# Attention, then two mixture-of-experts layers, on one core: the first head pair in halves, unread products, one gather by indirect DMA, and reads and loads in another order

## The chip, the cores and the metric

The kernel runs on one core of a Trainium2 chip. The metric is the device time of one execution in microseconds; the figure for a kernel is the median of its runs. The engines are named as the profile names them: PE (matrix products; PEld are its weight loads), DVE (vector), ACT (activations), POOL (GpSimd), SP (starts most of the DMAs). Each runs its own list of instructions in the order in which it is written, and waits where an input is not there yet.

## The reference

Three stages follow each other; the output of one is the input of the next.

```
scores = q @ k.T / 8                          # B=2, H=8, S=576, D=64, f32
scores = where(i // 64 >= j // 64, scores, -1e9)
attn   = exp(scores - max) / (sum + 1e-9);  x = attn @ v       # rows of 8*64 = 512
# MoE 1: N=1152 rows, E=8 experts, F=1024, capacity 288: one expert per row
e = argmax(x @ w_gate); slot = rank of the row among those of e, kept if below 288
x = gate_w * (relu(disp @ w1[e]) @ w2[e]), back in the row's place, else 0
# MoE 2: two experts per row, by noisy logits
out = sum over the two of weight * (relu(x @ w1[e]) @ w2[e])
```

## The kernel before

**Attention.** The 8 heads of a batch go in pairs, so there are 8 pairs (`pr`), and a pair's 576 rows are cut into tiles of 128 (the last has 64 rows of both heads). `turn_ops` turns a pair's q and k around on PE (line 442, and 479 for the last rows), ACT writes the rounded half of each (450, 487), DVE the remainder (459, 456, 492), and a copy of the rounded half goes into the other 64 partitions (466 by DMA; for the first pair 468 on ACT and 470 on POOL). These lie in `W[pr % 2]`, the tiles `both`, with a part that stands for the mask. `tile_ops` makes scores (526, 531), maxima on DVE (537 to 542), exponentials on ACT (550, 552), turns them (562, 558), copies them out (421 on DVE or 423 on ACT) and multiplies with v (608, 623). `fin_ops` ends a pair: it divides by the sums, writes the rows (`xrow`, lines 664, 667, 702) and the pair's share of the router's logits (674 to 694).

**Router and first rows.** `gate_ops(b)` takes a batch's logits (`g0`, 739 to 748), counts ranks on PE (`gp`, 752 to 757), places the rows (763 to 773), and enters row numbers into the table `T1` by one-hot products (`cells1` 797, `table` 806, `keep` 810). The first 128 rows of expert 0 are taken without a DMA: for each of the 5 tiles of rows of both batches PE multiplies `xrow` with a one-hot `choice` (779), 4 products a tile (`rows_in`, 822); all add up in one bank, which ACT and DVE split (858, 859). All rows also go to `x_d` in DRAM (`store`, 405, 406): batch 0 in one piece, batch 1 in columns 0 to 383 and then the rest.

**Weights.** Each expert's weights come in 8 units of 512 KB through a few raw buffers (`load`, 156, 159, on SP's queue); `split` makes two halves of a unit, rounded on ACT (167) and remainder on DVE (170, two instructions). Eleven units are split inside the attention; a split frees its raw buffer, and the load of a later unit goes out behind it on SP. One unit per expert stays whole (`wf`).

**Order in the attention.** `Weave` is a planner that runs when the kernel is built: `add` enters operations with cost, dependencies and the buffers they take, and `run` simulates the engines and picks the next operation by a score with the weights in the table `ATT` (line 22) and a random tie-break (`seed`, `noise`). What it writes is each engine's order; on the chip only semaphores decide when things run. MoE stages have a planner of their own (`Flow`).

**MoE 1.** `row1(e, blk)` gathers up to 128 rows of expert `e` from `x_d` by an indirect DMA on POOL (1441), for experts 0 and 1 ahead of the loop, later from inside it. `prep` turns the rows (1015) and splits them (1018, 1021). Here expert 0 takes the branch for at most 128 rows (`one_block`), which reads its rows from the bank above, and of its gathered rows only the columns behind the data.

**MoE 2.** `arm(e)` computes two blocks of 128 rows of expert `e`, and beside them prepares the next: `next_rows` and `rows2` gather (1418) into `g`. The output is read back, added to and written again: `prev` (1577) is an indirect DMA from `out`, `to_out` adds (1583) and scatters (1586). At the end of the program's list the loop is:

```
    for e in range(1, E):
        for blk in range(2):
            prev(G[e, blk][1], blk)
        arm(e)
        if e + 1 < E:
            with tc.If(many["n"] > 256):
                rest(e)
```

`rest(e)` is run for experts with more than 256 rows; in the trace that is one of them.

## Time and profile before

| | |
|---|---|
| median of 3 runs | 559.38 us (557.72 to 559.82) |
| profiled execution: time, span | 557.14 us, 555.5 us |
| mean granted PE clock | 0.992 |
| PE busy | 517.0 us (93%) |
| DVE / ACT / POOL busy | 378.9 (68%) / 294.1 (53%) / 138.4 us (25%) |
| read from and written to DRAM | 87.5 and 12.3 MB, 180 GB/s |

The time of an execution is a little over its span, which counts from the first to the last instruction of the core. PE is the engine with the most work; from about 14 us on it is busy in nearly every slice of the page but the eleventh and the thirty-sixth, so what counts are the places at which PE stands still and the work that it need not do. The timeline gives start, duration, engine, line, operation, and in brackets how long the engine had been idle and what ended that.

### The profile page before, as it was taken

How to read it: one execution, taken by the hardware profiler on the slowest of the kernel's cores; microseconds unless marked ns; L12 is line 12 of the kernel's file. 1: busy time of each engine (PE TensorE's matmuls, PEld its weight loads, DVE VectorE, ACT ScalarE, POOL GpSimd, SP SyncE). 2: the span in 40 equal slices, each digit the busy share in tenths (PEclk: the TensorE clock that was granted, in tenths of full speed). 3: DMA queues.
4: the chain of work that ended last, by engine and by line, in shares of the span. 5: the costliest groups of instructions: out<-in, count | busy, mean ns of one | idle time of the engine just before them, and what ended most of it. 6: DMA issues, size and time to landing. Idle time of an engine off the chain costs nothing. (4 is left out here: it accounts for less than half of the span.)

```text
span 555.5 us, 10106 instructions
## 1 busy us (share of the span) xinstructions
PE 517.0 (93%) x3381; PEld 422.8 (76%) x3381; DVE 378.9 (68%) x1008; ACT 294.1 (53%) x580; POOL 138.4 (25%) x225
## 2 busy tenths in 40 slices
PE   3999999999869999999999999989999999969996
PEld 3778777878647776787976967888989886949794
DVE  7899988888548988757674678464848562917441
ACT  5888878871347687544533536252635442716130
POOL 3000000000462234405233133142513132514131
PEclk9999999999999999999999999999999999979999
DMA  6998896423458878754632442638658591545220
GB/s 136 221 240 229 220 230 188 123 77 109 137 176 290 265 240 296 232 189 138 206 133 64 170 137 71 226 125 284 221 205 280 188 327 48 187 180 165 86 66 35
DMA packets 71176, 99.17 MB, mean 179 GB/s; under 512 B 37130, under 2 KB 40586, under 8 KB 71088
## 3 DMA queue, kind: packets, MB, share of 16 engines
q1 hardware_dynamic: 63600, 83.16, 47.6%
q0 software_dynamic: 6432, 14.71, 8.4%
q8 instruction: 39, 0.64, 0.5%
q14 instruction: 49, 0.40, 0.2%
q10 hardware_dynamic: 1056, 0.26, 0.2%
HBM read 87.53 MB, written 12.25 MB: 180 GB/s over the span
## 5 line engine op out<-in xcount | busy, mean ns | idle before, releaser
L170 DVE TENSOR_TENSOR wl<-raw,wh 128x512 fp32r<-128x512 f32 x140 | 91.6, 685 | 12.0 <-ACT wh L167 11.6
L167 ACT ACTIVATE wh<-raw 128x1024 fp32r<-128x1024 f32 x70 | 71.1, 1052 | 20.1 <-PEq L1780 12.5
L170 DVE TENSOR_TENSOR both<-raw,both 128x512 fp32r<-128x512 f32 x100 | 66.0, 684 | 8.9 <-ACT both L167 8.4
L167 ACT ACTIVATE both<-raw 128x1024 fp32r<-128x1024 f32 x50 | 51.3, 1054 | 10.0 <-PEq L1780 8.3
L198 PE MATMUL h<-xh,wh 128*128 128x256 f32 (+1 forms) x184 | 52.9, 287 | 0.5
L199 PE MATMUL h<-xl,wh 128*128 128x256 f32 (+1 forms) x184 | 52.6, 286 | 0.0
L200 PE MATMUL h<-xh,wl 128*128 128x256 f32 (+1 forms) x184 | 52.5, 285 | 0.0
L1018 ACT ACTIVATE xh<-tp 128x512 fp32r<-128x512 f32 (+1 forms) x37 | 19.0, 536 | 59.0 <-PE tp L1015 57.3
L1021 DVE TENSOR_TENSOR xl<-tp,xh 128x512 fp32r<-128x512 f32 (+1 forms) x37 | 21.9, 610 | 35.3 <-ACT xh L1018 35.1
L1145 ACT ACTIVATE hh<-h 128x512 fp32r<-128x512 f32 (+1 forms) x46 | 24.1, 523 | 38.7 <-PE h L200 32.3
L1586 POOL DMA_INDIRECT out_dram<-o,T2i x16 | 18.5, 1156 | 96.9 <-DVE o L1583 94.8
L1148 DVE SCALAR_TENSOR_TENSOR hl<-h,hh 128x512 fp32r<-128x512 f32 (+1 forms) x46 | 27.5, 597 | 22.1 <-ACT hh L1145 18.0
L198 PE MATMUL h<-xh,both 128*128 128x256 f32 (+1 forms) x136 | 39.2, 288 | 2.7 <-DVE hl L1148 1.4
L199 PE MATMUL h<-xl,both 128*128 128x256 f32 (+1 forms) x136 | 39.0, 287 | 0.0
L200 PE MATMUL h<-xh,both 128*128 128x256 f32 (+1 forms) x136 | 38.8, 285 | 0.0
L198 PE MATMUL y<-wh,hh 128*128 128x512 f32 (+1 forms) x94 | 38.3, 407 | 0.0
L200 PE MATMUL y<-wh,hl 128*128 128x512 f32 (+1 forms) x94 | 37.1, 394 | 0.0
L199 PE MATMUL y<-wl,hh 128*128 128x512 f32 (+1 forms) x94 | 36.9, 393 | 0.0
L550 ACT ACTIVATE pt<-s,negmax 128x128 f32<-128x128 f32 (+3 forms) x64 | 33.4, 526 | 6.4 <-DVE negmax L537 5.1
L526 PE MATMUL s<-both 128*128 128x256 f32 (+2 forms) x128 | 33.1, 371 | 3.8 <-ACT both L468 2.5
L198 PEld LDWEIGHTS h<-xh,wh 128*128 128x128 f32 x184 | 34.7, 189 | 2.1 <-issue 1.6
L199 PEld LDWEIGHTS h<-xl,wh 128*128 128x128 f32 x184 | 34.6, 188 | 0.0
(295 smaller groups left out, 1297.9 us busy)
## 6 DMA issues: line engine op xcount, KB each, us to landing
raw<-in_moe_w_dram SPq DMA_DIRECT2D x120, 512.0 KB, 5.1
wf<-in_moe_w_dram SPq DMA_DIRECT2D x8, 512.0 KB, 5.8
out_dram<-zero SPq DMA_DIRECT2D x3, 768.0 KB, 5.5
both<-both SPq DMA_DIRECT2D x14, 160.0 KB, 2.6
raw<-in_q_dram SPq DMA_DIRECT2D x16, 128.0 KB, 4.2
vn<-in_v_dram SPq DMA_DIRECT2D x16, 128.0 KB, 2.6
both<-both SPq DMA_DIRECT2D x14, 144.0 KB, 3.3
raw<-in_k_dram SPq DMA_DIRECT2D x14, 128.0 KB, 4.7
```

What stands on the lines that cost most here:

```text
L167: nc.scalar.activation(h, t, AF.Copy)
L170: (nc.gpsimd if part == 3 else nc.vector).tensor_sub(l[:, c], t[:, c], h[:, c].bitcast(F32))
L198: nc.tensor.matmul(o, sh, mh, start=first, stop=False)
L199: nc.tensor.matmul(o, sh, ml, start=False, stop=False)
L200: nc.tensor.matmul(o, sl, mh, start=False, stop=last)
L526: nc.tensor.matmul(o, w[:, i, h, 128 * t:128 * t + 128], w[:, i + 2, h, 64 * h:64 * h + n], start=(i == 0), stop=(i == 1))
L550: nc.scalar.activation(o, i, AF.Exp, bias=negmax[:, pr, 2 * t + h:2 * t + h + 1], accum_out=ssum[b][:, t, 2 * p + h:2 * p + h + 1])
L1018: nc.scalar.activation(xh[:, :, c0:c0 + n], h["tp"][:, :, :n], AF.Copy)
L1021: nc.vector.tensor_tensor(xl[:, :, c0:c0 + n], h["tp"][:, :, :n], xh[:, :, c0:c0 + n].bitcast(F32), op=OP.subtract)
L1145: nc.scalar.activation(part(hfull[0], g - (KF - 2 * WHOLE) // per) if plain(g) else part(hh, g), of(g), AF.Relu)
L1148: nc.vector.scalar_tensor_tensor(part(hl, g), of(g), 0.0, part(hh, g).bitcast(F32), op0=OP.max, op1=OP.subtract)
L1586: ins = nc.gpsimd.indirect_dma_start(out=out, out_offset=_off(G[key][1][:n, 0:1]), in_=G[key, "o"][:n], in_offset=None, bounds_check=NT - ...
```

## The change

The table `ATT` has other weights and another seed, the planner's costs and lags are set anew, and so the whole order of the attention moves. Beside that:

- *First pair.* Its q and k are loaded in halves of 256 rows (k on SP, q on ACT's queue), turned, split and copied half by half; the copies run on ACT or DVE, none on POOL. Scores of the first two tiles need only the first halves. The masks come from a pattern that POOL writes directly, without two ACT instructions; most small constants are made on POOL.
- *Unread products.* 56 bf16 products of a tile of ones go to PE into a bank that nobody reads, ahead of and between the first pair's steps.
- *First rows.* Batch 0's part of expert 0's first 128 rows is fetched from `x_d` by an indirect DMA (it waits for the store and for the table of batch 0) and enters the bank by 4 products with the identity.
- *Late loads.* Loads of units from the sixth on wait behind the store of batch 1.
- *Gathers and reads.* `row1` runs in the order (1,0), (0,1), (0,2), (1,1), (1,2), (0,0). `prev` of MoE 2 enters the planner's list inside `arm`.

```diff
-ATT = dict(P=0.024, A=0, V=0.122, G=0.074, beta=0, fit=0.3348, seed=13885, noise=0.1383, ...
+ATT = dict(P=0.076, A=0.0803, V=0.2935, G=0.2811, beta=0, fit=0.4128, seed=81227, noise=0.1133, ...
+UNREAD = 56
...
-                    queue = max(queue, op["end"] + 1.3) + op["dma"]
-                    op["end"] = queue + 1.0
+                    queue = max(queue, t + 1.5) + op["dma"]
+                    op["end"] = max(queue, op["end"] + 1.3) + 0.7
...
+            if b == p == 0:
+                for c in range(2):
+                    for i, src, e in ((1, k, nc.sync), (0, q, nc.scalar)):
+                        for hh in range(2):
+                            e.dma_start(out=qn[:, i, 2 * c:2 * c + 2, hh, :], in_=src[b, hh, 256 * c:256 * c + 256, :].rearrange("(c p) d -> p c d", p=128))
...
-        for x, m in enumerate((-31.5, -95.5)):
-            nc.gpsimd.memset(mid[:, x:x + 1], m)
-            nc.scalar.activation(near[x], jq, AF.Square, bias=mid[:, x:x + 1])
...
+            for g in range(2):
+                for x in (1, 0):
+                    main(x, 2 * g, 2)
+                made["W", pr, g] = list(res)
             a2 = tail()
+            res.append(AT.add("dup", "AV", dict(A=0.9, V=0.7), dup_tail, [a2]))
...
-                S_ = AT.add("s", "P", cost, scores, made["W", pr], ["s"])
+                S_ = AT.add("s", "P", cost, scores, made["W", pr, t // 2] if t < 4 else made["W", pr], ["s"])
...
+                def at(op):
+                    nc.gpsimd.tensor_scalar(rows0_at, T1f[:, 0:1, 0], float(NT), None, op0=OP.add)
+
+                def fetch(op):
+                    nc.gpsimd.indirect_dma_start(out=rows0, out_offset=None, in_=x_d[0:S], in_offset=_off(rows0_at[:, 0:1]), bounds_check=S - 1, oob_is_err=False)
+
+                st = AT.add("load", "S", 0.9, lambda op: store(0, slice(0, XW)), rows + [wt, made["gates"]], dma=3.8)
+                i0 = made["at"] = AT.add("fetch", "G", 0.2, at, [made["keep", 0]])
+                made["fetch"] = AT.add("fetch", "G", 1.2, fetch, [i0, st], dma=1.5)
...
+            def early(op):
+                for kk in range(KD):
+                    nc.tensor.matmul(bank(op, "s").rearrange("p (k n) -> p k n", n=128)[:, kk], rows0[:, kk * 128:kk * 128 + 128], ident,
+                                     start=(kk == 0), stop=False)
...
-            made["raw", i + RAWS] = AT.add("load", "S", 0.1, lambda op: load(behind(u)), [made["split", i]], dma=1.5, drawn=False)
+            made["raw", i + RAWS] = AT.add("load", "S", 0.1, lambda op: load(behind(u)), made["split", i], dma=1.5, drawn=False, behind=[made["stored"]] if i >= HELD else ())
...
+        def unread(op):
+            nc.tensor.matmul(rings["av"][0][:, 0:128], ones, ones, start=True, stop=True)
...
-    for blk, n in BLK:
-        row1(0, blk, n)
-
-    for blk, n in BLK:
-        row1(1, blk, n)
+    for e, i in ((1, 0), (0, 1), (0, 2), (1, 1), (1, 2), (0, 0)):
+        row1(e, *BLK[i])
...
-        blocks(F, E + e, xT[e % 2], 0, lambda y, blk, p, first: to_out(F, y, (e, blk), blk, p, first), done=done, apart=e + 1 == E)
+        before_ = [F.add("G", 1.04, lambda blk=blk: prev(G[e, blk][1], blk), after=3.5 if e + 1 < E else 0.0) for blk in range(2)]
+        blocks(F, E + e, xT[e % 2], 0, lambda y, blk, p, first: to_out(F, y, (e, blk), blk, p, first, deps=[before_[blk]]), done=done, apart=e + 1 == E)
...
-        for blk in range(2):
-            prev(G[e, blk][1], blk)
         arm(e)
```

Past the attention PE, DVE and ACT have the same instructions in the same order; POOL's order differs in `row1` and in six of the seven arms, SP's not at all.

On PE, at the end of the attention, before: the products with `choice` of batch 0 (line 822, `xrow_125`) stand between the last pair's closing steps (674 to 687 and 652), one tile of rows (x4) or two (x8) at a time.

```order
L822 MATMUL s_201<-choice_223,xrow_125 128x128 x4
L674 MATMUL tp_205<-xt_218,wblk 32x128 x4
L675 MATMUL tp_205<-xt_218,wblk 32x64
L676 MATMUL tp_205<-s4s,eye_165 64x2
L677 MATMUL tp_205<-ident,xt_218 64x128
L822 MATMUL s_201<-choice_223,xrow_125 128x128 x4
L686 MATMUL tp_205<-ident,lt_186 128x128
L687 MATMUL tp_205<-ident,lt_186 64x32
L652 MATMUL tp_206<-ident,xt_217 128x128 x4
L652 MATMUL tp_204<-ident,xt_218 128x128 x4
L822 MATMUL s_201<-choice_223,xrow_125 128x128 x8
```

The same place of the changed kernel (its lines 695 to 708 and 673 are those steps):

```order
L695 MATMUL tp_201<-xt_214,wblk 32x128 x4
L696 MATMUL tp_201<-xt_214,wblk 32x64
L697 MATMUL tp_201<-s4s,eye_166 64x2
L698 MATMUL tp_201<-ident,xt_214 64x128
L673 MATMUL tp_200<-ident,xt_214 128x128 x4
L673 MATMUL tp_202<-ident,xt_213 128x128 x4
L707 MATMUL tp_201<-ident,lt_182 128x128
L708 MATMUL tp_201<-ident,lt_182 64x32
```

Nothing of batch 0's rows stands between these steps now; the table of batch 0 is entered just ahead of them, and the 4 products with the fetched rows stand behind the ranks of batch 1.

On SP, at the same place, before: `raw` is a weight load, `x_d` the store of the rows of batch 1 (`xrow_124`), `wf` the unit that stays whole.

```order
L159 DMA raw_68<-in_moe_w_dram 128x2x512
L156 DMA raw_69<-in_moe_w_dram 128x1024
L156 DMA raw_70<-in_moe_w_dram 128x1024
L405 DMA x_d<-xrow_124 128x4x384
L406 DMA x_d<-xrow_124 64x384
L156 DMA raw_71<-in_moe_w_dram 128x1024
L156 DMA raw_67<-in_moe_w_dram 128x1024
L405 DMA x_d<-xrow_124 128x4x140
L406 DMA x_d<-xrow_124 64x140
L159 DMA wf_1746<-in_moe_w_dram 128x2x512
```

And in the changed kernel:

```order
L406 DMA x_d<-xrow_122 128x4x384
L407 DMA x_d<-xrow_122 64x384
L406 DMA x_d<-xrow_122 128x4x140
L407 DMA x_d<-xrow_122 64x140
L158 DMA raw_68<-in_moe_w_dram 128x2x512
L155 DMA raw_69<-in_moe_w_dram 128x1024
L155 DMA raw_70<-in_moe_w_dram 128x1024
L155 DMA raw_71<-in_moe_w_dram 128x1024
L155 DMA raw_67<-in_moe_w_dram 128x1024
L158 DMA wf_1804<-in_moe_w_dram 128x2x512
```

All five loads stand behind the whole store; before, three stood ahead of its first piece and two more ahead of its second.

On POOL, in an arm of MoE 2, before: `px<-out_dram` are the two reads of `prev`, `g<-x_d` the gathers for the next block of rows, `out_dram<-o` the scatters.

```order
L1577 DMA px_1732<-out_dram,T2i 128x512
L1577 DMA px_1733<-out_dram,T2i 128x512
L1418 DMA g_1740<-x_d,T2i 128x524
L1418 DMA g_1741<-x_d,T2i 128x524
L1418 DMA g_1742<-x_d,T2i 32x524
L1386 TENSOR_LOAD cnt_92
L1586 DMA out_dram<-o_6630,T2i 1152x512
L1586 DMA out_dram<-o_6631,T2i 1152x512
```

And in the changed kernel:

```order
L1461 DMA g_1798<-x_d,T2i 128x524
L1461 DMA g_1799<-x_d,T2i 128x524
L1461 DMA g_1800<-x_d,T2i 32x524
L1617 DMA px_1790<-out_dram,T2i 128x512
L1617 DMA px_1791<-out_dram,T2i 128x512
L1429 TENSOR_LOAD cnt_90
L1626 DMA out_dram<-o_6688,T2i 1152x512
L1626 DMA out_dram<-o_6689,T2i 1152x512
```

The three gathers stand ahead of the two reads in the six arms that have gathers.

## Rows read from the trace of the kernel before

**Rows 1.** Windows: stretch, length, busy by engine (instructions), PEclk, DMA share, GB/s

```profile
0.00:20.00 20.00, 11.41 (x57) 9.74 (x57) 14.11 (x43) 12.88 (x30) 5.00 (x29) 1.00 0.68 145
20.00:120.00 100.00, 97.01 (x841) 76.64 (x839) 89.62 (x209) 84.83 (x231) 0.00 (x0) 1.00 0.75 197
120.00:141.28 21.28, 19.82 (x197) 16.89 (x194) 18.48 (x66) 6.00 (x16) 0.10 (x1) 1.00 0.39 122
141.28:162.00 20.72, 14.48 (x67) 10.38 (x68) 9.61 (x21) 6.78 (x11) 11.88 (x19) 1.00 0.47 151
```

**Rows 2.** Waits of PE: who waited for whom, us in total, times, longest

```profile
PE tp L1015 <- DMA g<-x_d,T2i: 5.0, 2, 4.6
PE tp L1015 <- DMA xr<-x_d,T: 4.4, 2, 2.3
...
PE tp L562 <- ACT pT L423: 0.4, 1, 0.4
```

**Rows 3.** Timeline of the first pair, 5 to 14 us, PE and ACT

```profile
5.39 1.94 PE L442 MATMUL tp<-ident,raw 128*128 128x128 f32 x8 [5.39 <-DMA raw<-in_k_dram]
6.52 1.20 ACT L450 ACTIVATE both<-tp 64x512 fp32r<-64x512 f32 x2 [1.87 <-PE tp L442]
...
7.80 0.57 ACT L487 ACTIVATE both<-tp 64x128 fp32r<-64x128 f32 x2
...
9.50 1.48 ACT L468 ACTIVATE both<-both 64x640 fp32r<-64x640 f32 x2
...
10.28 2.48 PE L526 MATMUL s<-both 128*128 128x256 f32 x8 [2.52 <-ACT both L468]
```

**Rows 4.** Timeline of PE, the same products of a later pair

```profile
110.85 1.21 PE L526 MATMUL s<-both 128*128 128x256 f32 x8
```

**Rows 5.** Groups of PE by line in 120 to 133 us: x, busy, mean ns

```profile
L822 PE MATMUL s<-choice,xrow 128*128 128x128 f32 (+1 forms) x40 | 5.4, 279 | 0.0
```

**Rows 6.** Timeline of the attention's end, PE

```profile
130.46 2.14 PE L822 MATMUL s<-choice,xrow 128*128 128x128 f32 x16
132.53 0.20 PE L752 MATMUL tp<-oh,before 128*128 128x48 bf16 x1
...
134.41 4.92 PE L822 MATMUL s<-choice,xrow 128*128 128x128 f32 x40 [1.21 <-DVE choice L779]
```

**Rows 7.** Timeline of DVE, the last step ahead of the ranks

```profile
131.69 0.20 DVE L748 TENSOR_TENSOR oh<-real,ix 128x40 bf16<-128x40 f32 x1
```

**Rows 8.** Timeline of SP, ACT, POOL and PE, from the store to the first gathers

```profile
139.77 0.51 SPq L406 DMA_DIRECT2D x_d<-xrow  x1
...
146.21 0.60 ACT L1043 ACTIVATE yT<-h 128x512 f32<-128x512 f32 x1 [6.23 <-DMA x_d<-xrow]
...
147.03 1.22 POOL L1441 DMA_INDIRECT xr<-x_d,T  x1 [4.32 <-DMA wf<-in_moe_w_dram]
...
151.12 1.02 POOL L1441 DMA_INDIRECT xr<-x_d,T  x1 [0.31 <-issue]
152.44 1.48 POOL L1441 DMA_INDIRECT xr<-x_d,T  x1 [0.30 <-DVE wl L170]
...
146.86 0.66 PE L1048 MATMUL tp<-ident,yT 128*128 128x128 f32 x4 [1.86 <-ACT yT L1043]
155.09 0.65 PE L1015 MATMUL tp<-ident,xr 128*128 128x128 f32 x4 [2.26 <-DMA xr<-x_d,T]
158.78 0.63 PE L1015 MATMUL tp<-ident,xr 128*128 128x128 f32 x4 [2.11 <-DMA xr<-x_d,T]
```

**Rows 9.** Timeline of POOL and PE in the arm behind `rest`

```profile
481.15 1.84 POOL L1577 DMA_INDIRECT px<-out_dram,T2i  x1 [4.31 <-DMA out_dram<-o,T2i]
...
485.08 1.46 POOL L1418 DMA_INDIRECT g<-x_d,T2i  x1 [0.32 <-issue]
...
493.06 1.12 PE L1015 MATMUL tp<-ident,g 128*128 128x128 f32 x4 [4.64 <-DMA g<-x_d,T2i]
```

**Rows 10.** Window of PE behind that wait

```profile
493.00:498.00 5.00, 4.62 (x14) 3.28 (x14) 1.38 (x2) 1.20 (x2) 0.00 (x0) 0.50 0.07 27
```

## What I predicted before the run

> **What bounds the kernel now.** I read the windows of the attention and of what follows it first, then the table of PE's waits, then the timeline of each place at which PE stands. In 20 to 120 us PE is busy 97.0 of 100 us, against 76.6 (weight loads), 89.6 (DVE) and 84.8 (ACT) [rows 1]: there another order can win at most 3 us. PE loses time elsewhere: 8.6 us of the first 20, 1.5 of 21.3 in the attention's end and 6.2 of the 20.7 behind it [rows 1]. The table of waits names 5.0 us for gathered rows `g` in MoE 2, one of the two waits being 4.6, and 4.4 us in two waits for gathered rows `xr` [rows 2]. So a change at these places moves the end nearly one for one: behind the attention the order on PE, DVE and ACT stays, and what PE wins early it keeps unless something else comes late.
>
> **The first pair.** Before, the first turn starts at 5.39, when the k data land, and the first scores at 10.28: 4.89 us, in which ACT makes k's rounded half (two of 1.20 overlapping), the tail, q's half and the copy, in a row [rows 3]. PE's last wait there, 2.52, ends with that copy on ACT. With halves of 256 columns an activation should take between the 0.57 of the pair with 128 columns and the 1.20 of that with 512; I take 0.78, an estimate. Three of these (k half, q half, one copy; the other copy may lie on DVE) and about 0.9 of turning and of latency give 3.3 where 4.89 stood: 1.6 won. The halves have half the bytes and may land 0.5 to 1 before the 5.39, an estimate; I take 0.5. The first score products, 8 in 2.48 us [rows 3], took 1.21 at a later pair [rows 4], half as long: PE was at half speed, after standing idle. If the unread products keep it awake, up to 1.27 come back for these and something for the turns. Against it: 1.38 us of POOL's copying goes to ACT and DVE, shorter instructions cost a fixed part more each, and the second halves still have to be done before the third tile. I take 0.4 for the speed net of all this. Term 2.5, between -1 (the added instructions lie on the path) and 5 (the whole of 4.89 but the shortest possible, and the speed).
>
> The granted clock column shows 1.00 for 0 to 20 us [rows 1] though the products took twice their time, so for the start I trust the durations. In the window behind the long wait it does read 0.50 [rows 10], that is 1.2 of 2.4 GHz, after 4.64 us of idleness. The Trainium skill ("TensorE: Matmul & The Clock Gate", Part 1) says that the throttled state is the default and that activity releases it, so that unread products would count as well as read ones; the trace of before agrees with the first half (half speed at the start) and has nothing on the second. By that rule alone the start would gain the 1.27 and some of the turns.
>
> The 56 unread products cost nothing as long as PE waits anyway: 128 columns in bf16 against the 128x128 f32 products of 279 ns [rows 5] are at most 56 x 0.28 = 15.7 us of busy time at the very worst, in truth a fraction, and the last 14 of them stand ahead of the third tile's scores, at most 1 us if nothing else holds it up. The masks and constants go to POOL, which is busy 5.0 of 20 us [rows 1]; this idleness hides them. If a constant is late, the turns are late by it: inside the bound of -1.
>
> **The end of the attention.** Ahead of the ranks of batch 1, 40 products with `choice` go, 5.4 us [rows 5]; 4 products of 128x128 f32 with the identity come in, 8 records in the trace's count; at the rate of the 40 in 4.92 us, 0.12 each, they take 1.0 [rows 6]. Saved on PE: 4.4. But PE is not alone there: the ranks' input on DVE ended at 131.69 + 0.20 = 131.89 [rows 7], and the ranks started at 132.53 only because 16 of these products were before them [rows 6]: 0.6 is certain. What stands earlier between the closing steps fills waits of PE for DVE and ACT, which then show up as idleness. And batch 1's own 40 products still wait 1.21 for `choice` on DVE [rows 6]. The new order takes DVE's work of batch 0's `choice` (two instructions) off and puts batch 0's table ahead of the closing steps. I take 1.2, nearer to the certain end; bounds -3 and 4.1. The lower one is the fetch: table, `keep`, POOL's index, indirect DMA. Such a gather takes 155.09 - 151.12 = 3.97 from its start to the product that uses it and 158.78 - 152.44 = 6.34 with loads beside it [rows 8]; if it ends last, PE waits.
>
> **Store, loads and first gathers.** Three waits follow: 1.86 (ACT's step waited until 146.21 for the store begun at 139.77), 2.26 for the fourth gather, issued at 151.12, and 2.11 for the fifth, issued at 152.44 [rows 8]. The store moves ahead of five loads. Before, it took 146.21 - 139.77 = 6.4 with loads ahead of it; 1.9 less removes the first wait, and the gathers start about as much earlier. The one for (1,0) was fourth and is now first: 151.12 - 147.03 = 4.1 earlier beside that, so the 2.26 goes. (1,1) goes from fifth to fourth: 1.3 + 2, so about 0.6 less its flight; I keep the third wait at 2.9 to be careful, that is 0.6 to 0.8 worse. Sum 1.86 + 2.26 - 0.6 = 3.5; bounds 0 and 6.2 (all three). Late next: the loads now all lie behind the store and beside the gathers; the unit `wf` and the units that expert 0 and 1 take are later by up to the time of the three loads that stood ahead.
>
> **MoE 2's reads.** In the arm behind `rest`, the reads of `prev` stand ahead of the gathers on POOL and the first waits 4.31 us, until 481.15, for a scatter to `out`; the first gather goes at 485.08 and PE waits 4.64 until 493.06 [rows 9], then runs at clock 0.50 in 493 to 498, busy 4.62 [rows 10], half of which, 2.3, is excess. In the changed order the gathers need not wait for that scatter: they can go from 481.15 - 4.31 = 476.84 on, 8.2 earlier, while PE needs them 4.64 earlier. So 4.64, another 0.4 of the second wait [rows 2] and 2.3 go: 7.4 (0 to 7.4). Now `prev` is late instead: its two reads, 3.9 us from 481.15 to 485.08, stand behind three gathers and are needed only when the last products of a block are added, some 10 us on. The other arms' gathers were in time (PE has only these two waits in the table) and stay so.
>
> **The body of the attention.** New weights and seed give a new order; PE was busy 97 of 100 us, so 0, bounds -2.5 and 3.0.
>
> **Sum.** 2.5 + 1.2 + 3.5 + 7.4 + 0 = 14.6; 557.14 - 14.6 = 542.5. The profiled execution was 2.2 below the median of the runs, 559.38; I add half of that: 543.6.
>
> **Rivals.**
> - The unread products don't raise PE's speed, and the last 14 hold up the third tile: 0.4 and 1.0 go, the start gives 1.1, so 545.0. For it: the granted clock shows nothing to win.
> - The late loads collide with the gathers and the weights of expert 1 come late: the third term falls to 0, 547.1. For it: 6.34 against 3.97 for a gather beside loads [rows 8]. In the skill ("DMA: Bandwidth & Descriptors", "Issuing engines are not separate DMA queues") transfers interleave on the same 16 engines whoever starts them, which speaks against gaining by POOL's queue alone; by that rule the time would be 547.1 too, and the longer flight agrees.
> - The gathers of the arm aren't what PE waits for, or start late for another reason: the fourth term falls to 0, 551.0. Against it: the timeline's 8.2 us of room.
> - The fetched rows end last: the second term is -2.8, so 547.6.
> - Slower: the new order brings the chain maxima, exponentials, turning and copying out of a tile closer to its products, so that PE waits in each of 7 tiles x 8 pairs. The one wait of this kind that shows in before is 0.4 [rows 2]; 56 x 0.4 = 22.4 over the 14.6 won gives 543.6 + 22.4 = 566. It comes out slower than before by more than 0.5% from (562.2 - 543.6) / 56 = 0.33 us a tile on. Against it: the numbers of score and turning buffers stay, and 89.6 and 84.8 of 100 us on DVE and ACT [rows 1] leave them some room.
>
> **How the numbers follow.** Forecast 0.55, its own range 537 to 549 (start and gathers at either end); the clock 0.10; the collision 0.12; late gathers 0.08; the fetch last 0.08; the slow order 0.04. The range for all is 537 to 551. A measurement of this kernel can tell about 0.5%: 556.6 to 562.2 counts as no change. Everything but the last rival is below it, and 0.03 is left for several of them at once, which would come out within the 0.5%: faster 0.93, same 0.03, slower 0.04.
>
> **What would show it.** The first scores start near 8 us and 8 of their products take 1.2 to 1.5; in the window of the attention's body PE stays at 96 or more of 100; between the closing steps PE has gaps in place of the products of batch 0, and the ranks follow DVE's last step within 0.2; the store's landing is no one's wait, one wait for `xr` is left; in the arm behind `rest` the wait for `g` is gone and the clock stays 1.00. It is wrong if PE waits over 3 us for the fetched rows, if waits for weight loads appear in the first experts, or if POOL is so late with `prev` that DVE's adding holds up PE.

## The result, and the profile after

The changed kernel takes 550.94 us (median of 4 runs, 545.85 to 551.55); the kernel before, with one more run beside these, 558.55 (4 runs, 555.88 to 559.82). The ratio is 0.9865 (95% interval 0.983 to 0.9899): 7.6 us faster, where 543.6 had been forecast. The direction held and the size was about half. The profiled execution took 550.74 us against 557.14, its span 549.1 against 555.5: 6.4 less.

Both spans can be cut at the same events and compared stretch by stretch (times in us; the marks are PE's rows in the two timelines):

| stretch | before | after | difference | forecast |
|---|---|---|---|---|
| start to the first pair's last score products | 20.01 | 19.48 | -0.53 | -2.5 |
| body: to the last pair's last score products | 98.06 | 105.83 | **+7.77** | 0 |
| end of the attention: to expert 0's first product | 23.21 | 22.18 | -1.03 | -1.2 |
| expert 0's whole unit `wf`, and the first gathers | 18.44 | 12.76 | -5.68 | -3.5 |
| MoE 1 and MoE 2 up to the arm behind `rest` | 295.70 | 296.28 | +0.58 | 0 |
| that arm to the next | 64.73 | 57.17 | -7.56 | -7.4 |
| rest of the program | 35.35 | 35.40 | +0.05 | 0 |

Three stretches gave 14.3 us, 12.1 had been forecast for them; the body took 7.8 back. The windows of the changed kernel, cut at these marks, show how (columns as in [rows 1]: length, then each engine's busy time and count for PE, PEld, DVE, ACT, POOL, then granted clock, DMA share, GB/s):

```profile
0.00:19.48 19.48, 14.91 (x114) 12.46 (x114) 15.22 (x36) 14.47 (x38) 8.60 (x42) 0.91 0.59 131
19.48:125.31 105.83, 99.44 (x823) 77.32 (x822) 87.53 (x213) 81.30 (x219) 0.00 (x0) 0.95 0.70 184
125.31:147.49 22.18, 19.20 (x177) 16.59 (x178) 17.80 (x65) 9.50 (x23) 1.52 (x3) 0.92 0.23 64
147.49:160.25 12.76, 12.03 (x58) 9.51 (x59) 8.63 (x20) 6.05 (x10) 7.64 (x9) 1.00 0.87 310
456.53:513.70 57.17, 56.70 (x353) 47.20 (x352) 33.26 (x56) 25.53 (x37) 23.08 (x16) 1.00 0.52 178
```

The same stretch of the body in the kernel before:

```profile
20.01:118.07 98.06, 95.07 (x826) 74.91 (x823) 87.77 (x206) 83.19 (x227) 0.00 (x0) 1.00 0.76 201
```

PE does the same products in both (823 and 826 records). It stood still for 6.39 us instead of 2.99, which is 3.40; and it was busy for 99.44 us instead of 95.07, which is 4.37, at a mean granted clock of 0.95 instead of 1.00. DVE and ACT did no more than before. So the 7.77 are idle time and the slow clock behind it, in about equal parts. A second trace of the changed kernel (below) has 107.75 for this stretch, 9.7 more than before.

PE's waits in the whole changed program (us in total, times, longest), against [rows 2]:

```profile
PE s L547 <- DMA both<-both: 3.9, 4, 1.8
PE sm L1388 <- DVE C L1383: 3.7, 8, 0.7
PE s L547 <- ACT pt L571: 3.3, 5, 2.2
PE tp L776 <- DVE oh L772: 2.4, 1, 2.4
```

The waits for `g` and `xr` are gone, all of them. New at the top are score products that wait for `both<-both`: the DMAs that copy the rounded half of a pair's q and k into the other 64 partitions. PE's timeline at the fourth pair (start, duration, engine, line, operation; in brackets how long PE was idle and what ended it):

```profile
55.45 0.21 PE L708 MATMUL tp<-ident,lt 32*64 32x32 f32 x1
57.47 0.58 PE L547 MATMUL s<-both 128*128 128x256 f32 x1 [1.80 <-DMA both<-both]
58.76 1.86 PE L547 MATMUL s<-both 128*128 128x256 f32 x7 [0.71 <-DMA both<-both]
```

Why the copies came late stands in the list of SP's queue (SPq: time that the sequencer spent letting out the DMAs, and how many):

```profile
41.32 4.18 SPq L320 DMA_DIRECT2D raw<-in_q_dram  x2
45.53 1.28 SPq L320 DMA_DIRECT2D raw<-in_k_dram  x2
47.34 0.69 SPq L322 DMA_DIRECT2D q<-in_q_dram  x1
48.08 0.62 SPq L322 DMA_DIRECT2D q<-in_k_dram  x1
48.80 2.08 SPq L324 DMA_DIRECT2D vn<-in_v_dram  x2
50.98 0.60 SPq L325 DMA_DIRECT2D vn<-in_v_dram  x1
51.68 0.54 SPq L158 DMA_DIRECT2D raw<-in_moe_w_dram  x1
52.31 2.46 SPq L467 DMA_DIRECT2D both<-both  x4
```

And ACT's last step of what they copy, from its timeline:

```profile
47.48 0.55 ACT L502 ACTIVATE both<-tp 64x128 fp32r<-64x128 f32 x2
```

The fourth pair's data were ready at 48.03; its copies left SP from 52.31 on, behind all the loads of the fifth pair and one of a weight unit, PE stood from 55.67 and went on at 57.47. In the kernel before the copies of this pair stood behind the fifth pair's loads too, but SP got through these by 48.65:

```profile
41.29 1.89 SPq L319 DMA_DIRECT2D raw<-in_q_dram  x2
48.74 2.47 SPq L466 DMA_DIRECT2D both<-both  x4
```

There ACT's last step ended at 48.63 and PE came for the copies only at 56.97, 8.2 after the first left SP. In the changed order this room is 3.4. So the place in the list is not new; what changed is that SP needs 10.9 us instead of 7.4 to let out what stands ahead of the copies (the first two loads alone 4.18 instead of 1.89), and that PE comes 1.3 earlier. Why SP needs longer is not shown; from 38.15 on it had let out three weight units and a store of 768 KB, in the kernel before one unit and one such store in that time. Then the clock: one window at the second pair, and two around this wait.

```profile
20.00:30.00 10.00, 8.55 (x62) 6.74 (x63) 6.46 (x15) 7.62 (x20) 0.00 (x0) 0.83 1.05 270
50.00:60.00 10.00, 7.44 (x61) 5.97 (x61) 6.12 (x16) 6.35 (x15) 0.00 (x0) 0.86 0.87 213
60.00:70.00 10.00, 9.76 (x62) 7.49 (x62) 7.93 (x16) 7.33 (x22) 0.00 (x0) 0.80 0.75 204
```

From 60 to 70 us PE is busy for 9.76 of 10 (9.48 in the kernel before), but does 62 products in it; the kernel before does 77, and two traces below without that wait 85 and 94. A busy PE hides the loss: only the clock column (0.80, part of the time at 1.2 of 2.4 GHz) and the count show it. Between the last score products of successive pairs (first to second, second to third, and so on) the kernel before takes 15.9, 12.3, 16.4, 13.2, 15.6, 12.5, 12.1 us; the changed one 17.0, 13.9, 18.5, 17.1, 13.1, 14.3, 12.0.

The start, on PE's timeline:

```profile
1.20 2.42 PE L906 MATMUL av<-ones 128*128 128x128 bf16 x21 [1.20 <-DVE ones L85]
7.21 1.35 PE L547 MATMUL s<-both 128*128 128x256 f32 x8
8.62 0.94 PE L906 MATMUL av<-ones 128*128 128x128 bf16 x14
11.81 0.62 PE L547 MATMUL s<-both 128*128 128x384 f32 x2 [2.25 <-ACT pt L571]
```

The first scores start 3.07 earlier than in [rows 3] and take 1.35 where they took 2.48. Then PE stands for 2.25 until ACT has made the first exponentials: ACT, which has the second halves to round, did those first (until 10.93), and the exponentials from 10.95 on. In 13 to 16 us the granted clock is 0.50 in this trace. In the second trace of the same kernel it is 1.00 there, and the first pair's last scores start at 18.39, not at 19.48.

The end of the attention, PE:

```profile
137.21 0.20 PE L776 MATMUL tp<-oh,before 128*128 128x48 bf16 x1 [2.36 <-DVE oh L772]
137.50 1.14 PE L883 MATMUL s<-ident,rows 128*128 128x128 f32 x8
139.00 6.55 PE L846 MATMUL s<-choice,xrow 128*128 128x128 f32 x40 [0.36 <-DVE choice L803]
```

The fetched rows go in with 1.14 (1.0 forecast), and nothing waits for their DMA. The 40 products with `choice` (the trace has two records for each of 20) take 6.55 where they took 4.92 in [rows 6]. The mean clock of this stretch is 0.92, and PE stood for 2.36 a little ahead of them; in the second trace of this kernel they take 5.12 behind a wait of 2.35.

POOL's gathers in the arm behind `rest` now go first, and `prev` (line 1617) behind them:

```profile
475.01 2.92 POOL L1626 DMA_INDIRECT out_dram<-o,T2i  x1 [5.11 <-DVE o L1623]
478.23 2.24 POOL L1461 DMA_INDIRECT g<-x_d,T2i  x1 [0.30 <-issue]
480.77 3.28 POOL L1461 DMA_INDIRECT g<-x_d,T2i  x1 [0.30 <-issue]
484.36 1.41 POOL L1461 DMA_INDIRECT g<-x_d,T2i  x1 [0.30 <-PE h L199]
486.07 1.58 POOL L1617 DMA_INDIRECT px<-out_dram,T2i  x1 [0.30 <-issue]
```

The first gather starts at 478.23, in [rows 9] at 485.08; the arm itself starts 1.1 later than before, so the 476.84 of the forecast is 477.95 here, and it held within 0.3.

### The profile page after: what moved, and what is told of

Same layout as the page of the kernel before. It is cut to its first block, busy times and chain, and to the rows that moved or that the text cites. A ratio compares the mean times of both kernels' runs of the same rounds, so it can differ in the third digit from the quotient of the medians.

```text
span 549.1 us, 10185 instructions
## 1 busy us (share of the span) xinstructions
PE 519.5 (95%) x3405; PEld 424.8 (77%) x3405; DVE 377.2 (69%) x1003; ACT 295.8 (54%) x582; POOL 144.2 (26%) x240
## 5 line engine op out<-in xcount | busy, mean ns | idle before, releaser
L169 DVE TENSOR_TENSOR wl<-raw,wh 128x512 fp32r<-128x512 f32 x140 | 91.7, 685 | 11.7 <-ACT wh L166 10.9
L166 ACT ACTIVATE wh<-raw 128x1024 fp32r<-128x1024 f32 x70 | 71.4, 1053 | 19.8 <-PEq L1819 12.5
L1191 DVE SCALAR_TENSOR_TENSOR hl<-h,hh 128x512 fp32r<-128x512 f32 (+1 forms) x46 | 27.4, 597 | 19.2 <-ACT hh L1188 13.1
```

Source lines behind the costliest of these rows:

```text
L166: nc.scalar.activation(h, t, AF.Copy)
L169: (eng or (nc.gpsimd if part == 3 else nc.vector)).tensor_sub(l[:, c], t[:, c], h[:, c].bitcast(F32))
L1191: nc.vector.scalar_tensor_tensor(part(hl, g), of(g), 0.0, part(hh, g).bitcast(F32), op0=OP.max, op1=OP.subtract)
```

## The experiments

Times are medians with the range of the runs; ratios are to the kernel before on the same chip, with their 95% interval. "Expert 0" is the time at which its first product starts: 141.28 before, 147.49 after.

**The copies, all started by POOL.**

```diff
-                        nc.sync.dma_start(out=w[z, (0, 3)[x], h, d].bitcast(F32), ...
+                        nc.gpsimd.dma_start(out=w[z, (0, 3)[x], h, d].bitcast(F32), ...
```

> The changed kernel, in which the copies of the rounded halves (both<-both) are started by POOL, which does nothing in the attention, instead of standing in SP's list behind the next pair's loads. Theory A (the copies are late because they stand behind other transfers in SP's list, and PE's idleness then costs clock as well): PE's 3.9 us of waits for these copies fall under 0.8, the granted clock stays at 1.00 in 20 to 30 and 50 to 70 us, and the kernel takes 550.9 - 3.4 - 4.2 = about 543. Rival B (the copies are late because the 16 DMA engines are full there, share 0.87 to 1.05): the waits stay between 3 and 5 us and the time at 549 to 553.

Measured: 551.88 (551.47 to 553.5), ratio 0.9906 (0.9882 to 0.9929). The fourth pair's wait is gone and the clock is 1.00 from 50 to 70. But the second pair's is longer:

```profile
28.38 0.79 PE L547 MATMUL s<-both 128*128 128x256 f32 x2 [4.22 <-DMA both<-both]
```

Its copies started at 19.25, 0.6 earlier than in the changed kernel, and landed up to 9.1 us later, beside three loads of weights that SP let out from 19.82 on. In 15 to 110 us the copies of 144 KB take 5.4 from issue to landing in the median, 3.5 in the changed kernel. Expert 0 starts at 145.25, 2.2 earlier than in the change, and MoE then takes 2.7 more. So SP's list was the cause at the fourth pair. At the second an earlier start did not help; whether the loads beside them or POOL's own queue make the copies land so late is not told apart here. That wait varies anyway: in the traces in which SP starts these copies as in the change, from 19.4 to 20.1 on, the interval that ends with the second pair is 16.0 to 19.6, and 21.4 in one. The Trainium skill ("DMA: Bandwidth & Descriptors", "Issuing engines are not separate DMA queues") says that transfers interleave on the same engines whoever starts them, and that starting them elsewhere saves only the sequencer's time, usually small. The second pair is in keeping with the first half; at the fourth pair the sequencer's time, for the loads ahead of the copies, held these from 48.03 to 52.31, and 4.3 us are not small.

**The copies of POOL from the third pair on only.**

```diff
+                        (nc.sync if pr == 1 else nc.gpsimd).dma_start(out=w[z, (0, 3)[x], h, d].bitcast(F32), ...
```

> The changed kernel with the copies of the rounded halves started by POOL from the third pair on; the second pair's stay on SP, where in the run with all of them on POOL they only went out together with three weight loads. Theory A: the fourth pair's waits of 1.80 and 0.71 go and the half clock behind them, 2.7, so the first product of expert 0 comes at about 142.3 in place of 147.49; if nothing is given back behind that, the kernel takes 545.7, if it is given back as in the run with all copies on POOL, 548 to 550. Rival B (the copies are held up by the 16 DMA engines, not by SP's list): 147 and 551.

Measured: 548.18 (546.14 to 552.17), ratio 0.9861 (0.9813 to 0.9909). The window of the body:

```profile
19.48:118.74 99.26, 95.12 (x823) 74.18 (x822) 87.42 (x213) 81.07 (x219) 12.63 (x24) 1.00 0.74 196
```

99.26 where the change has 105.83 and the kernel before 98.06, with PE's busy time back to 95.12 and the clock to 1.00. Of the 6.6 won, 5.4 lie in the interval that ends with the fourth pair (18.5 to 13.1), and 1.0 at the second pair, whose copies are still SP's and happened to land earlier. Expert 0 starts at 140.82, 6.7 earlier than in the change; MoE then took 1.7 more (403.3 against 401.6). POOL lets the fourth pair's copies out from 47.02 on, SP had done so at 52.31. On the whole time nothing of this shows here: the ratio is that of the change (0.9865).

**The copies on SP, ahead of the next pair's loads.** The lists of the other engines stay as they are.

```diff
-            ... lambda op: (load_pair(b, p), load_wblk() if pr == 1 else None), deps, dma=4.4)
+            ... lambda op: made.update(late=(b, p)) if pr == 4 else (load_pair(b, p), load_wblk() if pr == 1 else None), deps, dma=4.4)
...
+                    made["copied", pr] = made.get(("copied", pr), 0) + 1
+                    if pr == 3 and made["copied", pr] == 2:
+                        load_pair(*made["late"])
```

> The changed kernel with one move on SP and none elsewhere: the fourth pair's copies go out ahead of the fifth pair's loads, not behind them; all five lists but SP's stay. Theory A (the place in SP's list is the cause): the fourth pair's waits and the half clock behind them go, the first product of expert 0 comes 4 to 6 us earlier than 147.5, the time is 3 to 6 us below the changed kernel's here. Rival B (the copies are late for the traffic on the DMA engines, or the fifth pair's loads come late in their place): no gain, a wait for raw in the fifth pair instead.

Measured: 552.33 (550.24 to 553.55), ratio 0.9887 (0.9855 to 0.9918). The interval that ends with the fourth pair falls from 18.5 to 13.1, its wait is gone. Behind the loads that were held back a later pair is late instead (the sixth pair's copies leave SP at 87.22, in the change at 83.49):

```profile
89.89 0.38 PE L550 MATMUL s<-both 128*128 128x256 f32 x1 [1.56 <-DMA both<-both]
91.27 1.01 PE L550 MATMUL s<-both 128*128 128x256 f32 x3 [1.00 <-DMA both<-both]
```

The interval that ends with the sixth pair is 18.0 where it was 13.1. The wait moved and cost as much as before; only another sequencer took it away. (The whole body is 110.09 in this trace: the second pair's copies, which the edit does not touch, landed later than in the change, 6.7 after their issue against 5.3.)

**Old order with `prev` inside the arm** (the kernel before, with this one part).

```diff
+        before_ = [F.add("G", 1.04, lambda blk=blk: prev(G[e, blk][1], blk), after=3.5 if e + 1 < E else 0.0) for blk in range(2)]
...
-        for blk in range(2):
-            prev(G[e, blk][1], blk)
```

> The kernel before with one part of the change alone: prev enters the planner's list inside the arm, so that the gathers stand ahead of its reads. Theory A (this term of the prediction was right): the wait of 4.64 for g and the clock of 0.50 behind it are gone, about 7.4 off the time, 558.6 to about 551.2. Rival B (the gain seen in the changed kernel there comes from its earlier changes, or the late prev gives it back): 556 to 559.

Measured: 549.59 (549.11 to 551.37), ratio 0.9863 (0.9838 to 0.9889): 7.8 us less than the 557.34 of the kernel before on this chip, with the wait for `g` gone. This part alone is worth as much as the whole change.

**The same and the late loads with the new order of `row1`.**

```diff
-            made["raw", i + RAWS] = AT.add("load", "S", 0.1, ..., [made["split", i]], dma=1.5, drawn=False)
+            made["raw", i + RAWS] = AT.add("load", "S", 0.1, ..., [made["split", i]], dma=1.5, drawn=False, behind=[made["stored"]] if i >= HELD else ())
...
+    for e, i in ((1, 0), (0, 1), (0, 2), (1, 1), (1, 2), (0, 0)):
+        row1(e, *BLK[i])
```

> The kernel before with its own attention, plus the moved prev, plus the late loads behind the store and the new order of the row1 gathers; nothing of the first pair, the unread products, the fetch or the table of weights. Theory A (the loss is in the new order of the attention and the two parts behind it are worth 7.5 and about 5.7): 558.6 - 13 = about 545.4, faster than the whole change by 5 us, with no wait over 1 us for xr, g or the store. Rival B (the waits behind the attention went only because the fetch and the earlier store of batch 0 come with the new order, or the late loads make weights late): 549 to 552.

Measured: 546.83 (545.45 to 548.63), ratio 0.9817 (0.9785 to 0.9849). Two of the change's parts, with the attention as it was, beat the whole. In its profiled execution the products with `choice` were slow (granted clock 0.74) behind the same wait of 1.21 behind which they took 4.92 in [rows 6]:

```profile
135.34 6.55 PE L822 MATMUL s<-choice,xrow 128*128 128x128 f32 x40 [1.21 <-DVE choice L779]
```

**Three of these again, on one chip, six runs each.** The change, the change with copies on POOL from the third pair on, and the old attention with the two parts behind it.

> The changed kernel itself, on the chip of the next three runs, so that they can be set against it: 549 to 552, the first product of expert 0 at 147.5, PE's waits for the fourth pair's copies 2 to 3 us.

> The run with the copies on POOL from the third pair on, once more beside the changed kernel: Theory A: 140.8 for the first product of expert 0 as in the first look, 2.5 to 5 us below the changed kernel here; Rival B: within 1.5 us of it, since the mixture-of-experts layers take back what the attention wins.

> The kernel before with the moved prev, the late loads and the order of row1, once more beside the changed kernel: the parts behind the attention without the new attention. Theory A (the new attention costs more than it brings): 3 to 5 us below the changed kernel here, 546 to 547. Rival B: within 1.5 us of it.

Measured: 551.98 (549.03 to 554.21), ratio 0.9882 (0.9844 to 0.9919); 548.93 (546.92 to 550.11), 0.9826 (0.9793 to 0.9859); 547.72 (546.1 to 548.79), 0.9812 (0.9781 to 0.9843). Expert 0 starts at 147.34, 143.81 and 141.66. The copies' queue makes 3.1 us of the whole time here, but the ranges overlap, and in the first runs the ratios were equal: in the body the gain is shown, in the whole time it is not beyond the noise. The changed attention as a whole costs 4.3, and here no run of the one reaches into the other's. The profiled body of the second repeat was longer than in its first run because the second pair's copies, which stay on SP, landed late (6.5 after their issue, 5.4 before): the interval from the first pair to the second was 19.3 there, 16.0 before, and is 17.0 and 18.4 in the two traces of the change itself. The `choice` products of the last kernel took 4.92 this time, behind the same 1.21:

```profile
134.80 4.92 PE L822 MATMUL s<-choice,xrow 128*128 128x128 f32 x40 [1.21 <-DVE choice L779]
```

That 1.6 did not stay: two waits for `xr`, 2.04 and 0.59, came back behind it, which the slower execution did not have. The old attention with the two parts is the fastest version found.

**Unread products left out, all else in the same order.**

```diff
         def unread(op):
-            nc.tensor.matmul(rings["av"][0][:, 0:128], ones, ones, start=True, stop=True)
+            pass
```

> The changed kernel without its 56 unread products; the order of all else stays. Theory A (they keep PE's clock up at the start, and that is worth what the prediction put at up to 1.27 us): the eight first score products take about 2.4 us in place of 1.35, the first product of expert 0 comes 1 to 2 us later than 147.49 and the kernel takes 552 to 553. Rival B (what the start won early it loses to ACT's second halves anyway: PE waits 2.25 us there for an exponential): the doubled products only shorten that wait, and the time stays at 550 to 551.5.

Measured: 556.22 (552.45 to 557.8), ratio 0.9972 (0.9948 to 0.9996). The first score products take longer:

```profile
7.13 2.06 PE L547 MATMUL s<-both 128*128 128x256 f32 x8
```

2.06 against 1.35: the unread products do raise PE's speed. But the first pair's last scores come at 19.50 (19.48 with them) and expert 0 starts at 147.35 (147.49): by then the 0.7 is worth nothing. The loss of this kernel arose later: from expert 0 on it takes 405.4 where the change takes 401.6, with a wait of 1.53 at 162.56 and this one in MoE 1, behind a branch:

```profile
264.67 0.39 PE L197 MATMUL h<-xh,both 128*128 128x288 f32 x1 [3.13 <-ACT both L166]
```

In the change PE waits 0.74 at this place. ACT's step is not what it waits for: there PE goes on at 262.09, while the same step runs until 263.52.

**Four, sixteen fewer, and sixteen more unread products.** The first two leave off the last of them (the lines below, with 40 in the second), the third sends the last one 17 times, 72 in all.

```diff
+            made["sent"] = made.get("sent", 0) + 1
+            if made.get("sent", 0) <= 52:
```

> The changed kernel with 4 of its 56 unread products left out at the end of their row, where PE waits 2.25 us anyway: PE's list is 8 rows shorter ahead of everything else, no work changes. Theory C (where a branch stands in an engine's list decides whether the engine stands still behind it): the first product of expert 0 stays at 147.4 within 0.3, and waits of 1 to 3 us with no other work behind them appear or not behind the branches between experts, in steps, so 549 to 555. Rival D (such waits come from what else runs at that moment): no new wait, 550 to 551.5.

> As with 52 products, with 16 left out and 32 rows less. Theory C: the attention's end at 147.4 within 0.4; the rest longer by 0 or by steps of 1 to 3 us at branches, other ones than with 52. Rival D: 550 to 551.5.

> As with 52 products, but 16 more than the 56, in the same wait of PE for ACT, 32 rows more; they may also keep the clock up that fell to 0.50 in 13 to 16 us, worth up to 0.5. Theory C: the attention's end at 146.5 to 147.5, the rest longer by 0 or by steps of 1 to 3 us at branches. Rival D: 550 to 551.

Measured: 551.08 (550.13 to 555.54, 5 runs), 551.42 (550.67 to 552.49, 3 runs) and 549.88 (549.78 and 549.98), ratios 0.9906, 0.9898 and 0.9868. The first has one wait of 1.95 marked "issue" that ends at 153.26, where the change has none (its profiled execution took 554.23); the other two have no wait marked so above 0.8 in MoE. So such waits are not in step with the length of the lists; with one trace each, it is not shown that the length matters at all. Expert 0 starts at 149.22, 147.63 and 149.17. In the first and the third the first pair's last scores came earlier (18.06 and 18.42 against 19.48), and PE then waited more for copies, 6.0 and 7.2 in all against 3.9: the second pair's copies set the pace there. The number of unread products is not the reason: the changed kernel itself does the same in its second trace (18.39, 6.1). In these three traces the clock is 1.00 in 13 to 16 us, in the first trace of the change and in the run with 40 it is 0.50 and 0.51.

**Unread products in the waits for the copies,** ahead of the first scores of the second and fourth pair.

```diff
+                            for _ in range({1: (6, 13), 3: (25, 10)}.get(pr, (0, 0))[h] if t == 0 else 0):
+                                nc.tensor.matmul(s[:, 256 * h:256 * h + 128], ones, ones, start=True, stop=True)
```

> The changed kernel with unread products put into PE's list just where it waits for the copies: 6 and 13 ahead of the first scores of the second pair's two heads, 25 and 10 ahead of those of the fourth pair. They go into the scores' own bank and are overwritten. The waits stay as long. Theory A (the idleness itself brings the clock down): the clock stays at 1.00 there, PE's products take their full-speed time, and 1.5 + 2.7 = 4.2 us of doubled durations are saved less 0.5 for products too many: about 547.2. Rival B (the clock falls for another reason, such as the heavy work ahead of it): the clock reads 0.50 in the same places and the time is 551 to 553.

Measured: 553.4 (551.73 to 554.68), ratio 0.9932 (0.9911 to 0.9952). The clock is 1.00 from 20 to 30 and from 50 to 70, the body 102.81 instead of 105.83, expert 0 starts 3.1 earlier. So the slow clock is a price of its own, beside the wait ahead of it. The whole is nevertheless slower than the change, because of waits in MoE such as

```profile
333.81 0.37 PE L1288 MATMUL tp<-ident,px 128*128 128x128 f32 x1 [1.94 <-issue]
```

behind which PE runs at half clock for 4 us and more (window, columns as above):

```profile
334.00:338.00 4.00, 4.00 (x15) 3.47 (x15) 2.11 (x7) 2.52 (x4) 1.08 (x1) 0.50 0.71 230
```

**Unread products in the old attention** (the kernel with the two parts behind it), 42 ahead of the first turn, 30 ahead of the first scores, 16 ahead of `choice`.

```diff
+                        for _ in range(42):
+                            nc.tensor.matmul(bank(op, "tp")[:, 0:128], ones, ones, start=True, stop=True)
...
+                for _ in range(0 if b else 16):
+                    nc.tensor.matmul(bank(op, "tp")[:, 256:384], ones, ones, start=True, stop=True)
```

> The kernel before with the moved prev, the late loads and the order of row1 (the faster of the versions so far), and in its own order of the attention 88 unread products where PE stands idle: 42 ahead of the first turn, 30 ahead of the first scores, 16 after the ranks of batch 1, ahead of the products with choice. Theory A (idleness lowers the clock, and products nobody reads keep it): the first eight scores take 1.3 us in place of 2.47, the 40 products with choice 4.9 in place of 6.55, together 2.8 to 4 off: 546.8 to about 543.5, the fastest. Rival B (the clock there is not PE's to keep, or the time is given back in the mixture-of-experts layers, as where the waits for the copies were filled): 546 to 549.

Measured: 561.33 (555.48 to 562.54), ratio 1.0048 (1.0006 to 1.009). A miss, and not a clean trial. The 42 run at half speed themselves (4.66 us, until 5.86; the 30 behind them take 1.84), but the first turn starts as before, at 5.65. What is late are the first scores, 11.71 where they start at 10.54 without the unread products: in this build ACT's list has also changed, and the mask's two instructions (341) stand behind the first rounded half and run at 7.16, where they ran at 3.20. Expert 0 starts at 144.04 (141.66 in the repeat without them), and MoE then takes 12.3 more, in waits such as

```profile
266.48 0.60 PE L198 MATMUL h<-xh,both 128*128 128x288 f32 x1 [2.87 <-ACT both L167]
```

The `choice` products took 4.92; that they owe it to the 16 is not shown, since the same kernel has 4.92 without these in one of its two traces.

**The old table, costs and lags on the new parts.**

```diff
-ATT = dict(P=0.076, A=0.0803, V=0.2935, ..., seed=81227, ...
+ATT = dict(P=0.024, A=0, V=0.122, ..., seed=13885, ...
...
-                    res.append(AT.add("dup", "S", 1.2, dup, [A, a2], dma=0.9))
+                    res.append(AT.add("dup", "G", 2.08, dup, [A, a2], dma=0.9))
```

> The changed kernel planned with the table of weights, the costs, the lags and the model of transfers of the kernel before; all parts of the change remain, and the planner writes a third order. Theory A (the loss lies in the order that the new numbers write, not in the parts): the body from the first pair's last scores to the last pair's takes 98 to 100 us, as before, not 105.8; the first product of expert 0 comes at 140 to 143 and the kernel takes 544 to 547. Rival B (the new parts themselves, above all the copies and loads of the first pairs, hold up PE in any order): waits of over 3 us for copies remain, the body stays at 104 to 107 and the time at 549 to 553.

Measured: 554.57 (553.84 to 556.28), ratio 0.9949 (0.993 to 0.9967). The body takes 109.1, longer than in the change, with no wait for copies but with others:

```profile
25.00 1.12 PE L444 MATMUL tp<-ident,raw 128*128 128x128 f32 x4 [2.59 <-ACT big L424]
```

So the old numbers do not bring the old body back; with the new parts they plan worse. Whether the parts would lengthen any order, or only these two, one more order can't tell. Which wait an order ends in does not show in these numbers; it showed in the trace alone.

## Why the prediction was half right

**The step that failed** is the body: "New weights and seed give a new order; PE was busy 97 of 100 us, so 0, bounds -2.5 and 3.0." It measured +7.8, and 9.7 in the second trace. The reason given bounds one side only: with PE at 97 of 100 an order can win at most 3, but nothing in that row limits what it can lose. And the copies were not among the things weighed, since PE hardly waited for them before; how much room they had (8.2 us at the fourth pair) and how much the new order leaves them was not asked. The experiments show the cause of the larger part: wherever the fourth pair's copies no longer stood behind the loads on SP's list (four traces of three kernels), its interval fell from 18.5 to 13.1, which is 5.4 of the 7.8; moving them up within SP's list moved the wait to another pair. Of the remaining 2.4, 1.1 lies at the second pair (17.0 against 15.9) and varies from execution to execution with the landing of its copies; the rest is spread over the other intervals, with both signs.

**The size of a wait** was reckoned at its length. The rows for that lay in [rows 10], which the prediction used for MoE 2, where 2.3 of the 7.4 is slow clock. In the body the idle time was 3.4 and the slow clock behind it 4.4; with the waits filled with unread products the clock came back, though the copies came no earlier.

**The rival on the slower side** had the right kind of mechanism, an order that brings producer and consumer too close, but the wrong chain: it priced maxima and exponentials in every tile, where four waits for one DMA, and the clock, were enough. Between its 566 and the forecast nothing stood for an order that costs part of what the other parts win, which is what came about. The upper end of the range, 551, was set by late gathers, and these did not occur: that 550.94 lies just inside it is luck.

**The start** was sized at 2.5 and kept 0.5. The steps held one by one: first scores near 8 (7.21), 1.2 to 1.5 for eight of them (1.35), 0.78 for a rounding of 256 columns (0.78, for two instructions in a row; the 1.20 of [rows 3] are two in a row as well, not two side by side). What was not followed is what stands next: ACT's second halves ahead of the first exponentials (2.25 of waiting). Nor was the clock, which fell behind that wait in one trace of two: with 1.00 in 13 to 16 us the first pair ends at 18.39, 1.6 earlier than before. That wins little, since the second pair's copies come next: expert 0 starts at 147.34 there, against 147.49. The rival by which the unread products don't raise the speed was wrong (2.06 without, 1.35 with), and yet 0.7 more there is worth nothing at the pair's end.

**The end of the attention** came out at 1.03 against 1.2, with the price of the early products right, the fetch nobody's wait, and ranks that start when DVE's last step allows. That the sum came out so close is luck: up to the first of the 40 `choice` products the stretch had won 2.65 (13.69 from its mark, 16.34 before), and these products lost 1.63 of it to the clock.

**Store, loads and gathers** gave 5.68 against 3.5: the third wait, kept in the sum out of care, went as well. (The two waits for `xr` lie in the twelfth slice of the page before, a 6; the eleventh is an 8.) The rival by which late loads collide with gathers did not come about in this trace; small waits for `xr` do return in others, 0.9 in the second trace of the change and 2.6 in one of the two with the old attention.

**MoE 2's reads** gave 7.56 against 7.4, by the mechanism foretold, and 7.8 alone. The last two terms together, 10.9, were measured at 10.1 (557.83 to 547.72) with the old attention; the rest of the change, forecast to win 3.7, costs 4.3. Its parts (the halves, the unread products, the fetched rows) were not run alone on the old order.

**Open** is why MoE takes time back in some of the kernels, while the code there is the same. A part of it is what one kernel varies by: from expert 0 on the change takes 401.6 in its first trace and 404.3 in its second. In the three traces with copies on POOL's queue (403.3 to 404.4) PE waits there 1.5 to 1.9 for `yT` and 0.8 to 0.9 for `hl` in line 1123, for which it waits 0.2 and not at all in the change's first trace. In four other kernels there are nine waits of 1.2 to 3.1 us, several of them just behind the branches between experts, put down to "issue" or to ACT. The Trainium skill ("Runtime: NRT & Kernel Launch", "Instruction fetch mechanics") says that a taken branch to a page outside the window held has to fetch it first. The traces bear on this: their DMA rows have two queues of kind "instruction", with 88 packets in the span of the change, and during each of the nine waits at least one such packet is under way. In the wait of 3.13 shown above, from 261.54 to 264.67, two packets run from 261.82 to 263.94; at the same place of the change they start at 262.56 and 262.91, and PE had gone on at 262.09. This fits fetches and does not show them: no run moves a fetch by itself, and the wait of 1.95 stands in the middle of an expert's products, not behind a branch.

## What to carry to other kernels

A busy share near 100% bounds what a new order can win, never what it can lose: before forecasting "no change" for a reordered stretch, look on each queue for small DMAs that someone waits for behind large loads that no one waits for yet, and compare the time they are ready with the time they are let out. Price a wait of PE twice, once for its length and once for what the clock column and the count of products show behind it. Where a change has parts in separate stretches, run them apart: here two small ones gave more than the whole.

## What the runs showed of the hardware

The same 1.21 us wait ahead of the same 40 products left PE at full speed in one execution of a kernel (4.92, granted clock 1.00) and slow in another (6.55, clock 0.74); a forecast can give such a place a chance, not a number. During the first microseconds the granted clock does not tell the speed: the column reads 1.00 in 5 to 10 us for eight score products that took 2.06 without unread products and for the same that took 1.35 behind them. SP's queue spent 0.5 to 2.1 us on letting out each DMA, 10.9 us on ten loads in a row (41.32 to 52.22), and these kept a copy that was ready waiting for 4.3 us.
